# Attention by hash buckets and a gated spatial layer: new lengths and paces for the scheduler, and four heads by keys in place of two

## The chip, the core and the metric

The kernel runs on one core of one Trainium2 chip. Its engines are TensorE (PE, with its weight load PEld), VectorE (DVE), ScalarE (ACT), GpSimd (POOL) and SyncE (SP), which issues most of the DMAs. The metric is the device time of one execution in microseconds; lower is better. A profile is one execution taken by the hardware profiler; its span runs from the first to the last instruction of the program.

## The reference

Four batches, eight heads, 768 positions, 64 numbers per head. Each query and key gets a bucket from the signs of six projections, attention is allowed within a bucket, and the result goes through a feed-forward layer in which one half gates the other after a product over the positions.

```python
q_bits = (np.einsum('bhsd,dk->bhsk', q, proj) > 0)          # k likewise
mask = q_bucket[:, :, :, None] == k_bucket[:, :, None, :]
scores = scale * np.matmul(q, k.transpose(0, 1, 3, 2))
scores = np.where(mask, scores, -1000000000.0)
attn = softmax(scores)                                      # over the keys
x = (attn @ v).transpose(0, 2, 1, 3).reshape(B, S, H * D)   # B 4, S 768, H * D 512
h = np.maximum(x @ w_in, 0.0)                               # d_ff 1024
u, v = h[..., :512], h[..., 512:]
v_n = (v - mean(v)) / np.sqrt(var(v) + 1e-06)
v_s = np.einsum('ts,bsd->btd', w_spatial, v_n) + b_spatial[None, :, None]
return (u * v_s) @ w_out
```

## The kernel before

**Tiles and steps.** 32 heads make 16 pairs `p`, head `n = 2p + e`. A pair has six tiles of 128 positions, and a pair and a tile make one step `g`, 96 in all. `scores` issues the step's 16 matmuls (`sp`, L480): products of float16 halves and, last, the hash bits, which push scores outside the bucket down.

**A head by queries** (`by_queries`) has queries on the partitions. DVE copies the scores out with their row maximum (`low`, L509), ACT or POOL makes the bias (`bias`, `nb`), ACT takes the exponential (`exp`, L519) and rounds it to float16 (`half`, L523), DVE or POOL makes the rest in float16 (`rest`, L527), and a transpose by DMA on SP's queue turns the tile (`turn`, L531, `pt<-pp`) before `weighted` multiplies it with the values (`pv`, L637, 18 matmuls a tile).

**A head by keys** (`by_keys`, the heads in `WIDE`) has keys on the partitions: ACT takes the exponential from the scores in one go (L552), in float32, and `weighted` uses it as it stands (6 float32 products a tile, which the trace counts as 12 matmuls). There is no `low`, `half`, `rest` or transpose. But the maximum of each query has to be in the mask beforehand: `row_max` computes scores of the hashed float16 part once more on PE (`mx`, 24 matmuls a head), DVE reduces them (L584, 12 a head), `max_row` turns them on PE and moves them with a DMA of SP (L611, `hk<-mt`) into one row of the mask operand. The last four score matmuls of a pair's first step (`sp<-hk`) wait for that row.

**After a batch.** `normalize` scales a pair's result; a DMA transpose (L683, `xt<-xs`) turns it. When a batch's four pairs are done, `mlp_units` gives the feed-forward layer as groups of three matmuls each on PE: `vps` (v = x w_in), `ups` (u), `sps` (the product over positions), `ops` (the output). For the last batch `partial_units` (`vpp`, `upp`) does three of its pairs ahead of the fourth; `xp` is the PE transpose of the last pair. `weights()` loads and splits the layer's weights in 36 jobs, DMAs on SP's queue among them.

**What sets the order.** Every piece of work is an `Op` with an engine, a length `d`, a rank and what it waits for. `timetable` plays the whole program with these lengths: an engine that falls free takes the ready operation (ready within `LOOK`) of lowest rank. A tuple rank (step, x) goes before plain ranks; a plain rank below 8.9 counts from the current step, the feed-forward groups (9) come four steps behind. Scores of a step may not start before `begin`, which grows by `T_FIRST`, `T_KEYS`, `T_QUERIES` or `T_LAST` per step. Where PE would be idle for over 0.5 us, `fill` puts dummy matmuls (`warm`, L208) of 0.08 us each. `X` is added from one engine to the next, `LATE` and `LATE_D` before PE. Nothing of this runs on the chip: the outcome is one fixed sequence of instructions on each engine, and every engine takes its own in order.

```python
t = op("P", 1.5, go, *at["hl", p], *at["hk", p], on=[sc, held["hl", p], held["hk", p]], rank=(g, 0))
t.ready = begin
```

Of the kernel before, what the change touches and what calls it, by code (L numbers as in the profile page):

```python
# [14 lines left out]
ALU = mybir.AluOpType  # L15
# [3 lines left out]
P = 128  # L19
# [16 lines left out]
def lsh_attention_spatial_gating(  # L36
# [23 lines left out]
    WIDE = {4, 6}  # L60
# [14 lines left out]
    X = 0.15  # L75
    TURN = 1.92
    ops = []
# [27 lines left out]
    def op(e, d, fn, *after, on=(), rank=4, land=0.0, dma=0.0, need=None, gives=None, alone=False):  # L105
        o = Op(e, d, fn, rank, land, dma)
        o.need, o.gives, o.alone = need, gives, alone or "G" in e and fn.__name__ not in ("move", "bias")
        wait = [a for a in after if a is not None]
        for h in on:
            assert not h.closed  # L110
            if not h.users:
                wait += h.before
            h.users.append(o)
        for a in {id(a): a for a in wait}.values():
            a.then.append(o)
            o.left += 1
        return o
# [139 lines left out]
    def weights():  # L257
# [15 lines left out]
        for i, (src, dst, m, f, key) in enumerate(jobs):  # L273
            c = {}

            def fetch(src=src, m=m, i=i, c=c):
                if RB[i] < 2:
                    t = wk.tile([P, NF, HS], F16, tag=f"g{RB[i]}", name=f"raw{i}").rearrange("p a q -> p (a q)")
                else:
                    if i == 2:  # L280
                        st["raws"] = wk.tile([P, 2, S], F32, tag="u", bufs=UB, name="raws")
                    t = st["raws"][:, RB[i] - 2].bitcast(F16)
                c["raw"] = t[:, :m * (4 if src.dtype != F32 else 2)].bitcast(src.dtype)
                nc.sync.dma_start(out=c["raw"], in_=src)

            z = m / 256
            raw = buf(f"raw{RB[i]}", 1).new()
            hold_ = [raw] if RB[i] < 2 else [raw, raws]
            t = op("S", 0.6, fetch, on=hold_, dma=0.95 if src.dtype != F32 else 0.75, rank=R_W)
            t.ready = W_FROM - 6 + W_EVERY * i  # L290
            hold = hold_
            if src.dtype == F32:
                c["w"] = None
            else:
                def first(m=m, i=i, c=c):
                    raw = c["raw"]
# [52 lines left out]
    def urgent(p):  # L349

        return NT * p - (8 if keys(p) else 3)

    def hash_rows(p, *after):
# [22 lines left out]
        t = op("V", 0.62, bits, t, on=[g0], rank=(urgent(p), 2), gives="m")  # L376
        t = op("V", 0.3, scale, t, on=[g0, g1], rank=(urgent(p), 2), alone=True)
# [11 lines left out]
    def split_qk(p, *after):  # L389
# [3 lines left out]
        def high():  # L393
# [13 lines left out]
    def split_v(p, *after):  # L407
# [17 lines left out]
        at["vp", p] = op("V", 0.1 + 0.8 * z, low, t, on=[held["v", p], h], rank=(NT * p - 1, 4), alone=True)  # L425
# [57 lines left out]
    def scores(p, i, g, begin):  # L483
# [6 lines left out]
        t = op("P", 1.5, go, *at["hl", p], *at["hk", p], on=[sc, held["hl", p], held["hk", p]], rank=(g, 0))  # L490
# [5 lines left out]
    def by_queries(p, i, e, g, t, sc):  # L496
# [36 lines left out]
        t = op("V", 0.95, low, t, on=[sc, hx, held["nb", n], held["mr", n]], rank=(g, 0.1 + 0.1 * e))  # L533
        at["nb", n] = t = t1 = op("AG", BIAS, bias, t, on=[held["nb", n], held["mr", n]], rank=(g, 0.1 + 0.1 * e))
        t = op("A", 0.83, exp, t, on=[hx, held["nb", n]], rank=(g, 0.1 + 0.1 * e))
        t = op("A", 0.77, half, t, on=[hx, hp], rank=(g, 1 + e))
# [3 lines left out]
    def by_keys(p, i, e, g, t, sc):  # L540
# [21 lines left out]
        t = op("A", 0.75, exp, t, on=[sc, ht if wide_ else hx], rank=(g, 0.1 + 0.1 * e))  # L562
        if not wide_:
            t = op("A", 0.75, half, t, on=[hx, ht], rank=(g, 1 + e))
            t = t3 = op("VG", REST, rest, t, on=[hx, ht], rank=(g, 1 + e))
        at["pt", n, i] = t

    def row_max(p, i, c, *after):
# [8 lines left out]
        for e in ks:  # L577
# [8 lines left out]
            at["mx", 2 * p + e] = op("V", 0.55, high, t, on=[held["mx", 2 * p + e]], rank=R_MAX, gives="m")  # L586
# [55 lines left out]
    def normalize(n, g):  # L642
# [77 lines left out]
    POST = ("VG", (0.56, 1.0))  # L720
# [26 lines left out]
    def partial_units():  # L747
# [12 lines left out]
        for i in range(NT):  # L760
# [7 lines left out]
            def then(t, c, pool, i=i, copy=copy):  # L768
                at["vpart", i] = op("A", 0.5, lambda: copy(c), t, on=[hv_[i // 3]], rank=1, gives=pool)
# [11 lines left out]
    def mlp_units(b):  # L781
# [14 lines left out]
        def v_unit(i):  # L796
# [12 lines left out]
            def then(t, c, pool):  # L809
# [16 lines left out]
                if last:  # L826
                    t = op("V", 0.69, plus, t, at["vpart", i], on=[h, held["vpart"][i // 3]], rank=1, gives=pool)
                    t = op("A", 0.5, relu, t, on=[h], rank=1)
                else:
                    t = op("A", 0.5, relu, t, on=[h], rank=1, gives=pool)  # L830
                t = op("V", 0.9, stats, t, on=[h, hmv[i // 3]], rank=3)
# [7 lines left out]
        def norm(g, t):  # L839
# [22 lines left out]
            t = op("V", 0.6, newton, t, on=[hve, hr, hmv[g]], rank=3, alone=True)  # L862
            for j in range(3):
# [14 lines left out]
                z = op("A", 0.52, scale, t, on=[hv32[i], hve, hr], rank=3)  # L878
                z = op("A", 0.52, high, z, done.get("first"), on=[hv32[i], hvn[0]], rank=3)
                done.setdefault("first", z)  # L880
                done["vn", i] = op(*(("VG", (0.68, 1.17)) if last else ("G", 1.17)), low, z, on=[hv32[i], hvn[0]], rank=3)
# [3 lines left out]
        def u_unit(d, h):  # L885
# [9 lines left out]
            def then(t, c, pool):  # L895
# [9 lines left out]
                if part:  # L905
                    t = op("V", 0.54, plus, t, at["upart", d], on=[hu[h], held["upart"][d // 2]], rank=1, gives=pool)
                done["u", d, h] = op("A", 0.4, relu, t, done.get(("u", 0, h)), on=[hu[h]], rank=1, gives=None if part else pool)
# [3 lines left out]
        def s_unit(d, h):  # L911
# [7 lines left out]
            def then(t, c, pool):  # L919
# [14 lines left out]
                t = op("V", 0.55, first, t, at["bt"], on=[hy], rank=1, gives=pool)  # L934
# [9 lines left out]
        def o_unit(i):  # L944
# [5 lines left out]
            def then(t, c, pool):  # L950
# [6 lines left out]
                t = op("A", 0.5, copy, t, on=[ho], rank=1, gives=pool)  # L957
# [26 lines left out]
    W_FROM, W_EVERY = 20.0, 2.6  # L984
# [17 lines left out]
    for g in range(STEPS + LAG):  # L1002
# [101 lines left out]
```

## Time and profile before

| | us |
|---|---|
| median of 3 runs | 706.8 (703.88 to 711.1) |
| the profiled execution | 703.99 |
| its span | 702.2 |
| PE busy | 634.7 (90%), of it 56.0 in 825 `warm` matmuls |
| DVE busy | 519.7 (74%) |
| ACT busy | 502.4 (72%) |
| POOL busy | 271.5 (39%) |
| DMA queue of SP and ACT, 16 engines | 84.0% of the span |
| mean granted clock of PE | 0.983 |

Busy time counts from the first to the last moment of an instruction, without waiting; two instructions that overlap on an engine count once. [...] In a row of a group, behind the bar, stand the busy time in us, the mean length of one in ns, and the engine's idle time just before them with what ended it.

### The profile page before, as it was taken

The numbers are of one execution on the slowest core, as the hardware profiler recorded it, in microseconds if no ns is written. First come the engines' busy times: TensorE is split into PE (matmuls) and PEld (weight loads), VectorE is DVE, ScalarE is ACT, GpSimd is POOL, SyncE is SP. The second block draws the span as 40 slices with busy tenths as digits, with TensorE's granted clock in tenths as the row PEclk, the third lists the DMA queues.
The fourth block names the chain that finished last, engine by engine and source line by source line (L and its number), as shares of the span: only waits on it lengthen the run. The fifth ranks groups of instructions, "written<-read, shape, count | busy, mean of one in ns | idle before, by whom it ended". The sixth has DMA issues, their size and how long they took to land.

```text
span 702.2 us, 18439 instructions
## 1 busy us (share of the span) xinstructions
PE 634.7 (90%) x7475; PEld 394.9 (56%) x7475; DVE 519.7 (74%) x997; ACT 502.4 (72%) x822; POOL 271.5 (39%) x368
## 2 busy tenths in 40 slices
PE   5888699978879779899989899899999999999997
PEld 3565467765445565565555456564655565556553
DVE  5788697899687998887759787888897774255150
ACT  2879488888897889777757798878777994453212
POOL 4457645527742535581534262534152220010000
PEclk9989999999999899999999999999999999999999
DMA  6999996999999999999998999899989876000102
GB/s 194 190 194 189 212 180 149 200 187 217 204 213 215 188 215 155 187 193 180 190 192 143 198 195 203 154 220 161 232 167 177 146 123 107 0 31 16 46 1 90
DMA packets 326252, 113.29 MB, mean 161 GB/s; under 512 B 312984, under 2 KB 316056, under 8 KB 326168
## 3 DMA queue, kind: packets, MB, share of 16 engines
q1 hardware_dynamic: 322232, 110.98, 84.0%
q0 software_dynamic: 3840, 1.12, 0.9%
q8 instruction: 58, 0.95, 0.6%
q14 instruction: 26, 0.21, 0.1%
q10 hardware_dynamic: 96, 0.04, 0.0%
HBM read 27.94 MB, written 6.29 MB: 49 GB/s over the span
## 4 chain that ended last, share of the span: by engine, by line
PE 43%; ACT 19%; DMA 16%; DVE 9%; issue 8%; POOL 2%; SPq 2%; DVEq 0%; ACTq 0%; POOLq 0%
DMA pt<-pp 12%; PE sps L734 11%; ACT ex L519 7%; PE sp L480 7%; PE pv L637 7%; PE ops L734 7%; ACT pp L523 6%; DVE ex L509 5%; PE vps L734 4%; PE ups L734 3%; DVE pp L527 2%; PE vpp L734 2%; SPq L531 1%; POOL pp L527 1%; DMA raws<-w_sp 1%
## 5 line engine op out<-in xcount | busy, mean ns | idle before, releaser
L527 DVE TENSOR_TENSOR pp<-ex,pp 128x768 f16<-128x768 f32 x133 | 139.1, 1064 | 61.2 <-ACT pp L523 60.5
L519 ACT ACTIVATE ex<-ex,nb 128x768 f32<-128x768 f32 x180 | 167.5, 934 | 22.4 <-POOL nb L514 18.2
L509 DVE TENSOR_SCALAR_CACHE_REDUCE ex<-sp 128x768 f32<-128x768 f32 x180 | 165.3, 952 | 18.9 <-PE sp L480 14.0
L523 ACT CAST pp<-ex 128x768 f16<-128x768 f32 x180 | 144.6, 826 | 8.4 <-DMA pt<-pp 6.4
L637 PE MATMUL pv<-vp,pt 128*128 128x65 f16 x3240 | 126.3, 194 | 26.3 <-DMA pt<-pp 24.2
L637 PEld LDWEIGHTS <-pt 128*128 128x128 f16 x3240 | 112.8, 98 | 65.3 <-DMA pt<-pp 35.4
L480 PE MATMUL sp<-hl 64*128 64x384 f16 x1080 | 109.6, 328 | 13.8 <-DVE ex L509 13.0
L734 PE MATMUL sps<-ws,vn 128*128 128x384 f16 x576 | 102.4, 329 | 0.4 <-DVE sg L369 0.4
L527 POOL TENSOR_TENSOR pp<-ex,pp 128x768 f16<-128x768 f32 x47 | 77.5, 1655 | 39.6 <-ACT pp L523 32.8
L480 PEld LDWEIGHTS <-hl 64*128 64x128 f16 x1104 | 51.3, 95 | 62.2 <-issue 34.5
L514 POOL TENSOR_SCALAR nb<-mr 128x1 f32<-128x1 f32 x81 | 24.4, 301 | 142.7 <-DVE ex L509 115.7
L734 PEld LDWEIGHTS <-vn 128*128 128x128 f16 x576 | 54.2, 98 | 37.3 <-issue 4.5
L734 PE MATMUL ups<-xt,wi 128*128 128x384 f16 x348 | 63.9, 332 | 5.0 <-ACT vr L817 3.0
L734 PE MATMUL ops<-wo,g 128*128 128x512 f16 x288 | 66.5, 379 | 0.1
L384 POOL DMA_DIRECT2D hk<-sg x112 | 58.5, 529 | 16.1 <-issue 5.8
L734 PE MATMUL vps<-wi,xt 128*128 128x512 f16 x234 | 55.4, 379 | 2.1 <-ACT vr L817 2.1
L208 PE MATMUL warm<-ident 128*128 128x128 f16 x825 | 56.0, 224 | 0.0
L208 PEld LDWEIGHTS <-ident 128*128 128x128 f16 x825 | 48.7, 100 | 9.8 <-issue 9.3
L516 ACT ACTIVATE nb<-mr 128x1 f32<-128x1 f32 x99 | 19.4, 196 | 48.2 <-DVE ex L509 48.1
L734 PEld LDWEIGHTS <-wi 128*128 128x128 f16 x384 | 36.2, 99 | 29.5 <-issue 8.4
L480 PE MATMUL sp<-hk 63*128 63x384 f16 (+1 forms) x360 | 48.0, 327 | 4.5 <-DMA hk<-sg 1.8
L932 ACT CAST g<-sy 128x384 f16<-128x384 f32 x32 | 16.2, 508 | 41.4 <-DVE sy L936 41.1
(114 smaller groups left out, 743.1 us busy)
## 6 DMA issues: line engine op xcount, KB each, us to landing
qk<-kq SPq DMA_DIRECT2D x16, 768.0 KB
out<-o SPq DMA_DIRECT2D x24, 256.0 KB
v<-v SPq DMA_DIRECT2D x14, 384.0 KB
pt<-pp SPq DMA_TRANSPOSE x180
raw<-w_in SPq DMA_DIRECT2D x8, 256.0 KB
raws<-w_in SPq DMA_DIRECT2D x8, 256.0 KB
hk<-sg POOLq DMA_DIRECT2D x112, 9.0 KB, 3.6
raw<-w_sp SPq DMA_DIRECT2D x6, 192.0 KB
```

The source lines that it names most:

```text
L208: nc.tensor.matmul(b[:, :P], lhsT=ident, rhs=ident, start=True, stop=True)
L384: eng.dma_start(out=hkt(p)[D * e:D * e + 2 * NB, 1 - j // 2, (j % 2) * HS:(j % 2 + 1) * HS], in_=sg[1][32 * j + 16 * e:32 * j + 16 * e + 2 ...
L480: nc.tensor.matmul(ps[e][:, c - halves[0]], lhsT=src[r, l, rows], rhs=src[r, m, cs], start=(a == 0), stop=(a == len(passes) - 1))
L509: nc.vector.tensor_scalar(ex, st["sc", p, i][e], -float(2 ** 28), None, op0=ALU.max, op1=ALU.max, accum_out=st["mx", n][:, i:i + 1])
L514: nc.gpsimd.tensor_scalar(nb, mx, -ISQ, None, op0=ALU.mult)
L516: nc.scalar.activation(nb, mx, AF.Copy, scale=-ISQ)
L519: nc.scalar.activation(st["e32", n, i], st["e32", n, i], AF.Exp, bias=st["nb", n][:, i:i + 1], scale=ISQ)
L523: nc.scalar.copy(st["pp", n, i][:, 0], st["e32", n, i])
L527: eng.tensor_tensor(out=st["pp", n, i][:, 1], in0=st.pop(("e32", n, i)), in1=st["pp", n, i][:, 0], op=ALU.subtract)
L637: nc.tensor.matmul(o, lhsT=l, rhs=m, start=(i == 0 and k == 0), stop=(i == NT - 1 and k == len(todo_) - 1))
L734: nc.tensor.matmul(c[0], lhsT=l(), rhs=r(), start=(j == 0), stop=(j == len(products) - 1))
L932: nc.scalar.copy(gt[h][0][:, d], y[0])
```

## The change

- `WIDE` grows from heads 4 and 6 to heads 2, 4, 6 and 8: one head each of pairs 1 to 4, all in the first 30 steps.
- The lengths of nearly all operations are replaced. They were about the time an operation is busy; they are now the time until the engine's next operation (`low` 0.95 to 0.88, `half` 0.77 to 0.73, scores 1.5 to 1.42, weight products 0.55 to 0.47 and so on).
- The pace: `T_KEYS` 4.8 to 5.0, `T_QUERIES` 6.0 to 5.4, a new `T_THIRD` 6.1 for pairs 8 to 11, `T_LAST` 6.0 to 6.25, `START` 9.0 to 8.5.
- Weights: rank `R_W` 0.9 to 0.6 (a lower rank goes first), a job every 2.2 in place of 2.6. `R_QK`, `X`, `LATE`, `LATE_D` and `LOOK` change too.
- `LATER` shifts the rank of four kinds of operation by name: `relu`, `first`, `bias` and `turn`.
- `stats` now makes its tile when it is first needed, whichever of three tiles comes first.

```diff
-    WIDE = {4, 6}
+    WIDE = {2, 4, 6, 8}
...
-    X = 0.15
+    X = 0.14
     TURN = 1.92
+    LATER = {'relu': 0.1, 'first': -0.9, 'bias': -0.3, 'turn': 0.3}
...
     def op(e, d, fn, *after, on=(), rank=4, land=0.0, dma=0.0, need=None, gives=None, alone=False):
+        later = LATER.get(fn.__name__.strip("<>"), 0.0)
+        if not isinstance(rank, tuple):
+            rank = rank + later
+        elif rank[1]:
+            rank = (rank[0] + later, rank[1])
...
-        t = op("V", 0.95, low, t, on=[sc, hx, held["nb", n], held["mr", n]], rank=(g, 0.1 + 0.1 * e))
+        t = op("V", 0.88, low, t, on=[sc, hx, held["nb", n], held["mr", n]], rank=(g, 0.1 + 0.1 * e))
...
-                    if i % 3 == 0:
+                    if i // 3 not in mv:
...
-    T_FIRST, T_KEYS, T_QUERIES, T_LAST = 5.0, 4.8, 6.0, 6.0
-    START = 9.0
-    LOOK = 0.2
+    T_FIRST, T_KEYS, T_QUERIES, T_THIRD, T_LAST = 5.0, 5.0, 5.4, 6.1, 6.25
+    START = 8.5
+    LOOK = 0
     R_MAX = 0.3
-    R_QK = 0.95
-    REST, BIAS = (0.96, 1.68), (0.25, 0.25)
+    R_QK = 1.25
+    REST, BIAS = (0.88, 1.6), (0.22, 0.25)
     CROSS = {NP - 1}
-    R_W = 0.9
-    LATE, LATE_D = 0.5, 2.5
+    R_W = 0.6
+    LATE, LATE_D = 0.2, 2.0
...
-    W_FROM, W_EVERY = 20.0, 2.6
+    W_FROM, W_EVERY = 22.0, 2.2
...
-            begin += T_FIRST if p == 0 else T_KEYS if keys(p) else T_LAST if p >= NP - NPAIR else T_QUERIES
+            begin += T_FIRST if p == 0 else T_KEYS if keys(p) else T_LAST if p >= NP - NPAIR else T_THIRD if p >= NP - 2 * NPAIR else T_QUERIES
```

In the rows of the built order below, names carry their numbers: `pt1_4` is tile 4 of head 1, `sp8_0_0` the scores of pair 8, tile 0, first head, `sps0_0_0` a group of batch 0; the last number of a name only counts tiles.

SP's queue around the transposes of step 4 (`pt0_4`, `pt1_4`), before:

```order
L531 DMA_TRANSPOSE pt1_3_646<-pp1_3_557 128x12x128
L284 DMA raw4_690<-w_in 128x256
L332 DMA qk3_711<-kq 128x1536
L531 DMA_TRANSPOSE pt0_4_727<-pp0_4_649 128x12x128
L531 DMA_TRANSPOSE pt1_4_835<-pp1_4_685 128x12x128
L531 DMA_TRANSPOSE pt0_5_847<-pp0_5_749 128x12x128
L531 DMA_TRANSPOSE pt1_5_880<-pp1_5_772 128x12x128
L531 DMA_TRANSPOSE pt2_0_912<-pp2_0_870 128x12x128
```

And now:

```order
L537 DMA_TRANSPOSE pt1_3_604<-pp1_3_538 128x12x128
L537 DMA_TRANSPOSE pt0_4_638<-pp0_4_588 128x12x128
L537 DMA_TRANSPOSE pt1_4_697<-pp1_4_597 128x12x128
L338 DMA qk3_743<-kq 128x1536
L617 DMA ws1_80<-mt2_768 1x6x128
L537 DMA_TRANSPOSE pt0_5_794<-pp0_5_659 128x12x128
L537 DMA_TRANSPOSE pt1_5_854<-pp1_5_676 128x12x128
L290 DMA raw4_876<-w_in 128x256
```

The move of head 2's maxima (`ws1<-mt2`) is new and stands behind the transposes of step 4 and the load of pair 3 (`qk3`); a weight load and `qk3` no longer stand ahead of them, and pair 1 has one transpose a step (`pt3_0` without `pt2_0`).

SP's queue where the last weights (`w_sp`, `w_out`) are loaded, before, around steps 32 and 33 (heads 10 and 11):

```order
L284 DMA raw29_3419<-w_out 128x256
L284 DMA raws_311<-w_sp 128x384
L284 DMA raw32_3428<-w_out 128x256
L531 DMA_TRANSPOSE pt10_2_3439<-pp10_2_3417 128x12x128
L531 DMA_TRANSPOSE pt11_2_3466<-pp11_2_3425 128x12x128
L284 DMA raws_311<-w_out 128x256
L284 DMA raws_311<-w_sp 128x384
L683 DMA_TRANSPOSE xt4_3595<-xs4_3503 128x12x128
L531 DMA_TRANSPOSE pt10_3_3618<-pp10_3_3528 128x12x128
L531 DMA_TRANSPOSE pt11_3_3662<-pp11_3_3552 128x12x128
```

And now, around steps 26 to 28 (head 9 alone):

```order
L290 DMA raws_338<-w_sp 128x384
L290 DMA raw29_2573<-w_out 128x256
L290 DMA raw32_2598<-w_out 128x256
L689 DMA_TRANSPOSE xt3_2618<-xs3_2569 128x12x128
L537 DMA_TRANSPOSE pt9_2_2656<-pp9_2_2575 128x12x128
L290 DMA raws_338<-w_out 128x256 x2
L537 DMA_TRANSPOSE pt9_3_2715<-pp9_3_2680 128x12x128
L290 DMA raw33_2750<-w_out 128x256
L338 DMA qk6_2754<-kq 128x1536
L351 DMA v32_6_2781<-v 128x768
```

The last weight loads moved from among the transposes of two heads by queries to among those of one.

PE where the first group of the product over positions (`sps0_0_0`) begins, before: its first six matmuls stand ahead of step 48 (`sp8_0_0`); the last of them are

```order
L734 LDWEIGHTS vn0_0_4846
L734 MATMUL sps0_0_0_5095<-ws1_80,vn0_0_4846 128x384
L734 LDWEIGHTS vn0_1_4847
L734 MATMUL sps0_0_0_5095<-ws0_79,vn0_1_4847 128x384
L480 LDWEIGHTS hl8_4434
L480 MATMUL sp8_0_0_5106<-hl8_4434 128x384
```

And now, ahead of step 43 (`sp7_1_0`):

```order
L740 LDWEIGHTS vn0_0_3626
L740 MATMUL sps0_0_0_4114<-ws1_80,vn0_0_3626 128x384
L740 LDWEIGHTS vn0_1_3627
L740 MATMUL sps0_0_0_4114<-ws0_79,vn0_1_3627 128x384
L486 LDWEIGHTS hl7_3446
L486 MATMUL sp7_1_0_4119<-hl7_3446 128x384
```

The group starts five steps earlier. Over the whole order PE has these matmuls, counted in the same three parts (before, and after the change):

| | up to step 47 | steps 48 to 95 | behind the last scores |
|---|---|---|---|
| `warm` | 636, 178 (and 64, 66 ahead of step 0) | 69, 37 | 56, 18 |
| `mx` | 48, 96 | 0, 0 | 0, 0 |
| `pv` in float16 | 1422, 1206 | 1710, 1728 | 108, 90 |
| key tiles (`pv` in float32) | 12, 24 | 0, 0 | 0, 0 |
| `vps` and `vpp` | 72, 72 | 144, 162 | 72, 54 |
| `ups` and `upp` | 96, 96 | 162, 192 | 126, 96 |
| `sps` | 6, 72 | 282, 306 | 288, 198 |
| `ops` | 0, 0 | 144, 180 | 144, 108 |

More of the change, by code (lines that the diff above doesn't have):

```diff
@@ L375, in hash_rows @@
         t = op("P", 0.8, go, at["qk", p], *after, on=[qk], rank=(urgent(p), 3), need=("m", 1))
-        t = op("V", 0.62, bits, t, on=[g0], rank=(urgent(p), 2), gives="m")
-        t = op("V", 0.3, scale, t, on=[g0, g1], rank=(urgent(p), 2), alone=True)
+        t = op("V", 0.54, bits, t, on=[g0], rank=(urgent(p), 2), gives="m")
+        t = op("V", 0.24, scale, t, on=[g0, g1], rank=(urgent(p), 2), alone=True)
         at["hk", p] = []
@@ L424, in split_v @@
         t = op("A", 0.15 + 0.6 * z, high, at["v", p], *after, on=[held["v", p], h], rank=(NT * p - 1, 4))
-        at["vp", p] = op("V", 0.1 + 0.8 * z, low, t, on=[held["v", p], h], rank=(NT * p - 1, 4), alone=True)
+        at["vp", p] = op("V", 0.07 + 0.8 * z, low, t, on=[held["v", p], h], rank=(NT * p - 1, 4), alone=True)
     def mean_v(p, *after):
@@ L768, in then @@
             def then(t, c, pool, i=i, copy=copy):
-                at["vpart", i] = op("A", 0.5, lambda: copy(c), t, on=[hv_[i // 3]], rank=1, gives=pool)
+                at["vpart", i] = op("A", 0.49, lambda: copy(c), t, on=[hv_[i // 3]], rank=1, gives=pool)
             group(f"vpp{i}", F2, v_products(b, i, pairs), then, on, after, bank_m, rank=8.9)
@@ L861, in norm @@
             t = op("A", 0.45, root, t, on=[hve, hr], rank=3)
[L862 removed]
+            t = op("V", 0.67, newton, t, on=[hve, hr, hmv[g]], rank=3, alone=True)
             for j in range(3):
@@ L876, in low @@
                     eng.tensor_tensor(out=vn[1][:, i], in0=v32[i], in1=vn[0][:, i], op=ALU.subtract)
-                z = op("A", 0.52, scale, t, on=[hv32[i], hve, hr], rank=3)
+                z = op("A", 0.7, scale, t, on=[hv32[i], hve, hr], rank=3)
                 z = op("A", 0.52, high, z, done.get("first"), on=[hv32[i], hvn[0]], rank=3)
                 done.setdefault("first", z)
-                done["vn", i] = op(*(("VG", (0.68, 1.17)) if last else ("G", 1.17)), low, z, on=[hv32[i], hvn[0]], rank=3)
+                done["vn", i] = op(*(("VG", (0.6, 1.12)) if last else ("G", 1.12)), low, z, on=[hv32[i], hvn[0]], rank=3)
         hu, hg, gs = {}, {}, {}
@@ L905, in then @@
                 if part:
-                    t = op("V", 0.54, plus, t, at["upart", d], on=[hu[h], held["upart"][d // 2]], rank=1, gives=pool)
-                done["u", d, h] = op("A", 0.4, relu, t, done.get(("u", 0, h)), on=[hu[h]], rank=1, gives=None if part else pool)
+                    t = op("V", 0.48, plus, t, at["upart", d], on=[hu[h], held["upart"][d // 2]], rank=1, gives=pool)
+                done["u", d, h] = op("A", 0.38, relu, t, done.get(("u", 0, h)), on=[hu[h]], rank=1, gives=None if part else pool)
             group(f"ups{b}_{d}_{h}", HS, u_products(b, d, h, LASTP if part else ALLP), then, xts, ready + at["wu"], bank(), [hu[h]], 8.9 if last else 9)
@@ L932, in high @@
                     nc.scalar.copy(gt[h][0][:, d], y[0])
-                t = op("V", 0.55, first, t, at["bt"], on=[hy], rank=1, gives=pool)
+                t = op("V", 0.5, first, t, at["bt"], on=[hy], rank=1, gives=pool)
                 either = lambda o: nc.gpsimd if o.e == "G" else nc.vector
@@ L955, in copy @@
                     nc.scalar.activation(o[0], c[0], AF.Copy, scale=1.0 / (SX * SX))
-                t = op("A", 0.5, copy, t, on=[ho], rank=1, gives=pool)
+                t = op("A", 0.49, copy, t, on=[ho], rank=1, gives=pool)
                 op("S", 0.4, lambda: nc.sync.dma_start(out=out[b, i * P:(i + 1) * P, :], in_=o[0]), t, on=[ho], rank=2, dma=0.95)
```

48 lines of the change are left out of this document (24 added, 24 removed).

## The prediction

> **What bounds the kernel now.** The page of the profile comes first: how long the span is, and which engines the chain that ended last runs through.
>
> ```profile
> span 702.2 us, 18439 instructions
> PE 43%; ACT 19%; DMA 16%; DVE 9%; issue 8%; POOL 2%; SPq 2%; DVEq 0%; ACTq 0%; POOLq 0%
> ```
>
> No engine carries even half of the chain, so one bound for the whole span would be wrong. I therefore cut the span where the limits change. A step is one query tile of one pair of heads: 16 score matmuls, 96 steps. Counting those matmuls in the timeline of PE gives the first matmul of steps 0, 6 and 48 and the first and last rows of step 95:
>
> ```profile
> 12.76 1.15 PE L480 MATMUL sp<-hl 64*128 64x384 f16 x12
> 43.53 0.66 PE L480 MATMUL sp<-ws 64*128 64x384 f16 x6
> 289.61 0.32 PE L480 MATMUL sp<-hl 64*128 64x384 f16 x1 [1.44 <-DVE ex L509]
> 574.62 1.15 PE L480 MATMUL sp<-hl 64*128 64x384 f16 x12
> 575.61 0.49 PE L480 MATMUL sp<-hk 63*128 63x384 f16 x4
> ```
>
> Third, the view of windows, cut at those places (columns: stretch, length, busy time of PE, PEld, DVE, ACT, POOL, granted clock, DMA share, GB/s):
>
> ```profile
> 12.76:289.61 276.85, 231.87 (x3257) 160.79 (x3255) 231.84 (x456) 225.45 (x386) 147.84 (x187) 0.96 1.03 193
> 289.61:576.03 286.42, 274.21 (x3335) 160.66 (x3335) 230.22 (x431) 228.11 (x350) 114.83 (x162) 0.99 1.00 181
> 576.03:702.20 126.17, 121.64 (x808) 68.59 (x806) 48.95 (x99) 45.33 (x85) 5.04 (x5) 1.00 0.17 41
> ...
> 84.32:137.10 52.78, 49.41 (x625) 37.00 (x624) 42.91 (x92) 40.70 (x73) 27.71 (x33) 1.00 0.89 184
> 137.10:174.06 36.96, 31.72 (x460) 22.04 (x459) 35.87 (x66) 32.88 (x61) 16.75 (x22) 1.00 1.06 202
> 174.06:289.61 115.55, 94.35 (x1330) 62.03 (x1329) 96.97 (x188) 97.97 (x168) 57.89 (x77) 0.96 1.07 197
> ```
>
> Before step 48 DMA is the fullest resource (share 1.03), DVE is at 84% and ACT at 81%, and much of PE's 232 us is warm-up filler. From step 48 to the last scores PE is busy 274.2 of 286.4 us. After them PE is busy 121.6 of 126.2 us and DMA lies idle: 121.6 us of PE work stand in a tail that overlaps nothing else. In the last three rows the two pairs that have a key head today (steps 12 to 23) take 52.8/12 = 4.4 us a step at DMA share 0.89. The four pairs behind them take 6.2 and 6.4 us a step at 1.06 and 1.07.
>
> **Prices.** PE's prices come from the chain of waits, where a merged row gives the time per instruction:
>
> ```profile
> 73.15 0.78 PE hp L362 x8
> 98.06 1.48 PE pv L637 x12
> 103.75 0.65 PE mx L480 x4
> 481.89 1.20 PE pv L637 x36
> 619.23 1.79 PE warm L208 x32
> 643.77 7.80 PE ups L734 x48
> 651.58 7.77 PE ops L734 x36
> 659.34 17.55 PE sps L734 x108
> ```
>
> So: `mx`, `ups` and `sps` 0.163 us each, `ops` (and `vps`, `vpp`, equally wide) 0.216, `pv` 0.033, warm 0.056, and 1.48 us for the weighted sum of one key tile. The other engines' prices come from the groups, DMA's from the issues of the transposes (minimum, median, maximum ns):
>
> ```profile
> L519 ACT ACTIVATE ex<-ex,nb 128x768 f32<-128x768 f32 x180 | 167.5, 934 | 22.4 <-POOL nb L514 18.2
> L509 DVE TENSOR_SCALAR_CACHE_REDUCE ex<-sp 128x768 f32<-128x768 f32 x180 | 165.3, 952 | 18.9 <-PE sp L480 14.0 <-PE mx L480 3.7 <-POOL pp L527 0.8
> L523 ACT CAST pp<-ex 128x768 f16<-128x768 f32 x180 | 144.6, 826 | 8.4 <-DMA pt<-pp 6.4
> L527 DVE TENSOR_TENSOR pp<-ex,pp 128x768 f16<-128x768 f32 x133 | 139.1, 1064 | 61.2 <-ACT pp L523 60.5
> L584 DVE TENSOR_REDUCE mx<-mx 128x1 f32<-128x384 f32 x24 | 12.3, 548 | 0.6 <-PE mx L480 0.4
> L552 ACT ACTIVATE ex<-sp 128x768 f32<-128x768 f32 x12 | 9.7, 804 | 8.5 <-PE sp L480 8.5
> L531 SPq DMA_TRANSPOSE pt<-pp x180: 1317/1738/4457, 23.4 to 584.9; - x180
> ```
>
> **Part one, up to step 48.** Heads 2 and 8 go over to keys, so 12 tiles lose their `low`, `half`, `rest` and transpose. DVE saves 12 × 0.918 (165.3/180) and 8 × 1.06 us, and gains 24 maxima of 0.51: 7.2 us less. ACT loses 12 × (0.93 + 0.80), gains 12 × 0.81 and drops small biases: about 13 us less. DMA loses 12 transposes of 1.74 us: 20.9 us less. On PE the built order has, up to step 48: 48 more `mx` (+7.8), 12 key tiles more (+17.8) against 216 fewer `pv` (-7.2), 66 more `sps` (+10.7), 458 fewer warm matmuls (-25.6): +3.5 us in all, so real work takes the filler's place. Weight loads leave the queue by step 29 instead of step 38, so the stretch from 174 us on, the one with share 1.07, keeps only transposes and head loads.
>
> How much comes through? If DMA is the bound, all 20.9 us. If DVE is, then 7.2 less what comes early behind the 66 `sps` (3.7 evictions and their products, about 1.3 us each): 2.4 us. DMA's share of 1.03 against DVE's 0.84 is the stronger row, so I take 18 us for steps 6 to 47. The Trainium skill, page "DMA: Bandwidth & Descriptors", section "Latency and other measured facts", gives 261 GB/s for a DMA transpose: an estimate of 1.5 us for the 393 KB of one tile, and 18 us for twelve where the row's median makes 20.9. No run here shows a transpose alone, and the median of the row stands in the sum.
>
> Against that, step 6 gets a wait that only steps 12 and 18 have today: its mask needs the key head's maxima, moved through SP's queue. Today's wait at step 12 shows its size:
>
> ```profile
> 43.70 8.92 DMA pt<-pp
> ...
> 78.76 3.32 SPq L531
> 82.84 4.23 DMA hk<-mt
> ...
> 87.11 0.50 PE L480 MATMUL sp<-hk 64*128 64x384 f16 x4 [1.64 <-DMA hk<-mt]
> ```
>
> In the new order the scores of step 6 stand behind the weighted sums of step 4, whose transpose was issued at 43.70 and took 8.9 us, and the mask's move stands behind that transpose and a 768 KB load. Queued behind the waiting matmul are all scores of pair 1, hence ACT's and DVE's next work. With two loads fewer ahead of it I put step 6 at 50 us instead of 43.5: 6.5 us lost; 0 if the transposes land in 2 us, 9 with all of that landing. Step 48: 289.6 - 18 + 6.5 = 278.1, between 268.7 (289.6 - 20.9) and 296 (289.6 + 6.5).
>
> **Part two, steps 48 to 95.** The order has 36 more `ops` (+7.8), 24 more `sps` (+3.9), 30 more `ups` (+4.9), 18 `vpp` (+3.9), 18 `pv` (+0.6) and 32 fewer warm (-1.8): +19.3. PE's 274.2 becomes 293.5. Idle was 12.2 us; denser PE work covers more waits, so I take 9, bounds 4 and 12: 302.5 us, 297.5 to 305.7.
>
> **Part three, the tail.** What went forward is gone here: 90 `sps` (-14.6), 36 `ops` (-7.8), 30 `ups` (-4.9), 18 `vpp` (-3.9), 18 `pv` (-0.6), 38 warm (-2.1), so 121.6 becomes 87.7; 4.5 us of idle stay. But there is less to cover the last softmax:
>
> ```profile
> 576.97 3.35 SPq L531 DMA_TRANSPOSE pt<-pp  x2
> 583.39 3.28 SPq L531 DMA_TRANSPOSE pt<-pp  x2
> 591.51 0.71 PE L637 MATMUL pv<-vp,pt 128*128 128x65 f16 x18
> 594.33 0.50 PE L704 MATMUL xp<-ident,xs 128*128 128x128 f16 x6
> ```
>
> From the last scores (576.0) to `xp` (594.3) are 18.3 us; the new order has 90 `pv`, 36 `vpp` and 24 `upp` between them, 3.0 + 7.8 + 3.9 = 14.7 us. I add 3 us of new wait: 95.3 us, 92 to 99.
>
> **The small edits** (`LATER`, `LOOK`, `X`, new lengths) only choose among instructions that are ready; they remove none. I cost them at nothing, because in parts two and three PE's other matmuls hide the choice; where that cover is thin, up to step 48, their worth is inside the 2.4 to 20.9 us above, and below nothing it is the first rival.
>
> **Sum.** 278.1 + 302.5 + 95.3 = 675.9 us of span. The profiled execution took 703.99 us, 1.8 over its span: 677.7. The median shown, 706.8, is 1.004 times that execution: 680.
>
> **Rivals**, all on the median's scale.
>
> *DVE and ACT hold the first part.* Step 48 stays at 289.6: 12 us more, 692. For it: both are above 80% busy, in-order, and both already wait for one another; against it: the share of DMA, and 4.4 us a step where a key head runs. Chance 0.17.
>
> *All of DMA's relief comes through and step 6 loses nothing*: 268.7 + 299 + 93 + 1.8 = 662.5, times 1.004: 665. For it: the quick steps 12 to 23; against it: the landing of 8.9 us ahead of step 6. Chance 0.10.
>
> *PE's clock.* 458 of 636 filler matmuls go from part one, and where fill was thin the clock dipped:
>
> ```profile
> 30.00:40.00 10.00, 7.39 (x87) 5.44 (x89) 7.53 (x17) 9.02 (x13) 4.28 (x8) 0.66 1.09 202
> 230.00:240.00 10.00, 7.04 (x103) 5.11 (x104) 8.67 (x21) 8.79 (x17) 4.59 (x5) 0.66 0.80 176
> ```
>
> A dip costs 10 × 0.34 = 3.4 us of PE time. Seven more of them where PE is the bound give 680 + 24 = 704, no change. Against it: `sps` and key tiles now stand where the filler stood, and both dips lie where PE is not the bound. Chance 0.09. The Trainium skill, page "TensorE: Matmul & The Clock Gate", section "Part 1: The HAM clock gate", states that a window of about 3.4 us without enough matmul work puts the clock to half; the two rows agree (0.66 over 10 us is 6.8 us at half), and by that rule filler removed without replacement speaks against this change.
>
> *Slower: the key heads' starts.* Four pairs now begin with a mask that comes through maxima, a transpose on PE, a copy and SP's queue. If each start holds PE's in-order queue for 10 us (3.3 + 4.2 us above plus the copy), with nothing to make up for it, the four cost 40 us in place of the 6.5 I counted and part one gains nothing from its lighter load: 278 becomes about 316 and the time 718. It decides from some 27 us above my step 48, a time over 707. Against it: today step 12 waits 1.64 us at the mask itself and steps 12 to 23 then run at 4.4 us each. Chance 0.09.
>
> **Chances.** The forecast 0.55, the rivals 0.17, 0.10, 0.09, 0.09. About 1% (7 us) is what a measurement can tell from no change, so under 699.7 is faster. Faster: 0.55 + 0.17 + 0.10 = 0.82, of which I move 0.02 to same, for a first rival that comes with long waits in part two. Same: 0.11. Slower: 0.09. The range goes from just below the second rival, 663, to the upper bounds of parts one and two (296 + 305.7 + 99 + 1.8, times 1.004: 705); it leaves out the slow case and what lies at its ends.
>
> **What would show it.** Step 48's first scores near 278 us, step 6's near 50; DMA share under 1 up to about 170 us; PE busy over 96% from step 48 on; about 95 us after the last scores, with one wait of 2 to 4 us ahead of `xp`. A first matmul of step 48 after 300 us, or a tail above 105 us, would show me wrong.

## The result, and the profile after

The changed kernel takes 671.5 us (median; 669.12 to 673.13), the kernel before on the same chip 708.0 (703.88 to 711.1). The ratio is 0.9485, 95% interval 0.9426 to 0.9544: faster by 5.1%, where 680 us, a ratio of 0.962 (680/706.8), were forecast. The profiled execution took 673.13 us with a span of 671.4.

The page's span and chain, as they stand now:

```profile
span 671.4 us, 17301 instructions
PE 47%; DVE 16%; ACT 14%; DMA 13%; issue 6%; POOL 3%; SPq 1%; DVEq 0%; ACTq 0%; POOLq 0%
```

The first score matmul of steps 0, 6 and 48, and the last scores, in the timeline of PE:

```profile
14.12 1.15 PE L486 MATMUL sp<-hl 64*128 64x384 f16 x12
49.46 0.82 PE L486 MATMUL sp<-ws 64*128 64x384 f16 x8
283.56 1.15 PE L486 MATMUL sp<-hl 64*128 64x384 f16 x12
577.39 1.15 PE L486 MATMUL sp<-hl 64*128 64x384 f16 x12
578.38 0.49 PE L486 MATMUL sp<-hk 63*128 63x384 f16 x4
```

And the windows cut there, with the columns of the prediction's windows (stretch, length, busy PE, PEld, DVE, ACT, POOL, granted clock, DMA share, GB/s); the last four rows cut the first one up again, behind step 6, at steps 12, 24 and 30. The granted clock is the mean share of its full clock that PE was given; the share of DMA adds up the times of all packets, so it can pass 1:

```profile
14.12:283.56 269.44, 240.26 (x2846) 157.01 (x2846) 224.53 (x467) 216.26 (x375) 154.73 (x193) 0.94 0.93 180
283.56:578.80 295.24, 289.91 (x3431) 168.89 (x3430) 229.40 (x436) 232.81 (x355) 111.31 (x165) 1.00 1.00 181
578.80:671.40 92.60, 87.81 (x578) 48.93 (x576) 40.10 (x85) 36.54 (x68) 3.10 (x4) 0.99 0.17 42
...
49.46:80.08 30.62, 27.47 (x302) 18.50 (x301) 25.60 (x62) 20.98 (x38) 15.00 (x15) 0.89 0.82 169
80.08:149.72 69.64, 63.97 (x663) 44.78 (x662) 55.21 (x128) 49.91 (x93) 38.31 (x53) 0.88 0.84 167
149.72:180.76 31.04, 27.01 (x334) 19.52 (x333) 23.46 (x43) 28.42 (x53) 21.16 (x27) 1.00 0.87 202
180.76:283.56 102.80, 93.70 (x1164) 55.39 (x1163) 90.88 (x180) 90.03 (x150) 53.75 (x69) 0.98 1.04 185
```

Step 48 comes 6.0 us earlier (283.6 against 289.6), the stretch from there to the last scores is 8.8 us longer (295.2 against 286.4), and the tail is 33.6 us shorter (92.6 against 126.2): 30.8 us in all. PE's idle time in the middle stretch fell from 12.2 to 5.3 us. So the gain lies in the tail: PE does, while attention runs, much of what it used to do alone at the end. Attention itself ends 2.8 us later than before.

### The profile page after: what moved, and what is told of

Its sections match the earlier page's. It is cut to its first block, busy times and chain, and to the rows that moved or that the text cites. A ratio compares the mean times of both kernels' runs of the same rounds, so it can differ in the third digit from the quotient of the medians.

```text
span 671.4 us, 17301 instructions
## 1 busy us (share of the span) xinstructions
PE 626.3 (93%) x6931; PEld 381.0 (57%) x6931; DVE 502.7 (75%) x1000; ACT 489.1 (73%) x800; POOL 272.9 (41%) x375
## 4 chain that ended last, share of the span: by engine, by line
PE 47%; DVE 16%; ACT 14%; DMA 13%; issue 6%; POOL 3%; SPq 1%; DVEq 0%; ACTq 0%; POOLq 0%
PE sp L486 10%; PE pv L643 8%; PE sps L740 8%; PE ops L740 7%; DMA pt<-pp 7%; PE vps L740 5%; DVE ex L515 5%; ACT ex L525 4%; ACT pp L529 4%; DVE pp L533 3%; PE ups L740 3%; PE vpp L740 2%; DMA raw<-w_sp 2%; DVE hl L408 2%; PE mx L486 1%
## 5 line engine op out<-in xcount | busy, mean ns | idle before, releaser
L533 DVE TENSOR_TENSOR pp<-ex,pp 128x768 f16<-128x768 f32 x125 | 125.5, 1012 | 63.5 <-ACT pp L529 62.8
L515 DVE TENSOR_SCALAR_CACHE_REDUCE ex<-sp 128x768 f32<-128x768 f32 x168 | 154.7, 952 | 22.9 <-PE sp L486 22.8
L525 ACT ACTIVATE ex<-ex,nb 128x768 f32<-128x768 f32 x168 | 155.9, 933 | 12.5 <-POOL nb L520 9.6
L529 ACT CAST pp<-ex 128x768 f16<-128x768 f32 x168 | 137.4, 827 | 7.8 <-DMA pt<-pp 5.2
L643 PEld LDWEIGHTS <-pt 128*128 128x128 f16 x3024 | 107.7, 98 | 46.2 <-issue 21.5
L643 PE MATMUL pv<-vp,pt 128*128 128x65 f16 x3024 | 120.4, 194 | 7.1 <-DMA pt<-pp 7.1
L533 POOL TENSOR_TENSOR pp<-ex,pp 128x768 f16<-128x768 f32 x43 | 71.2, 1660 | 59.3 <-ACT pp L529 40.3
L486 PEld LDWEIGHTS <-hl 64*128 64x128 f16 x1116 | 53.3, 96 | 59.6 <-issue 32.3
L740 PEld LDWEIGHTS <-g 128*128 128x128 f16 x288 | 26.7, 98 | 31.0 <-issue 1.9
L740 PEld LDWEIGHTS <-xt 128*128 128x128 f16 x288 | 25.9, 98 | 30.3 <-issue 2.5
L643 PE MATMUL pv<-vf,ex 128*128 128x65 f32 x288 | 37.9, 283 | 3.3 <-ACT ex L558 3.2
```

Source lines behind the costliest of these rows:

```text
L486: nc.tensor.matmul(ps[e][:, c - halves[0]], lhsT=src[r, l, rows], rhs=src[r, m, cs], start=(a == 0), stop=(a == len(passes) - 1))
L515: nc.vector.tensor_scalar(ex, st["sc", p, i][e], -float(2 ** 28), None, op0=ALU.max, op1=ALU.max, accum_out=st["mx", n][:, i:i + 1])
L525: nc.scalar.activation(st["e32", n, i], st["e32", n, i], AF.Exp, bias=st["nb", n][:, i:i + 1], scale=ISQ)
L529: nc.scalar.copy(st["pp", n, i][:, 0], st["e32", n, i])
L533: eng.tensor_tensor(out=st["pp", n, i][:, 1], in0=st.pop(("e32", n, i)), in1=st["pp", n, i][:, 0], op=ALU.subtract)
L643: nc.tensor.matmul(o, lhsT=l, rhs=m, start=(i == 0 and k == 0), stop=(i == NT - 1 and k == len(todo_) - 1))
```

## What the runs were to tell apart

Theory 1 is the prediction's: the time is the start of step 48, plus PE's work from there on, plus what the order leaves behind the last scores. The rivals put the gain elsewhere: in the load that the two key heads take off DMA, DVE and ACT; in the paces; in nothing that the small edits do. A second question is the part of the sum that was uncertain from the start, what bounds steps 6 to 47.

The experiments with their median time, and the same terms read from each profile, in us. The last column is worked out from the built order alone: the matmuls behind the last scores at the prediction's prices, filler included, with 4.5 us of idle added. The medians come from three chips, on which the kernel before took 708.0, 707.3 and 706.0; ratios, below, are each to the runs of before on the same chip.

| | median | step 6 | step 48 | 48 to last scores | tail | tail from the order |
|---|---|---|---|---|---|---|
| before | 706.0 to 708.0 | 43.5 | 289.6 | 286.5 | 126.1 | 126 |
| changed | 671.5 | 49.5 | 283.6 | 295.3 | 92.5 | 92 |
| heads alone | 722.6 | 55.8 | 275.2 | 289.8 | 155.4 | 153 |
| two heads | 704.1 | 42.8 | 283.3 | 298.1 | 117.4 | 116 |
| without `LATER` | 677.7 | 57.7 | 280.1 | 296.8 | 103.2 | 103 |
| old paces | 675.1 | 53.3 | 285.8 | 287.8 | 102.1 | 101 |
| old margins | 696.7 | 52.2 | 273.4 | 297.7 | 123.0 | 120 |
| no filler | 674.9 | 48.4 | 284.7 | 295.5 | 92.4 | 91 |
| three heads | 685.8 | 42.7 | 282.9 | 296.0 | 103.8 | 103 |
| slower paces | 683.7 | 49.7 | 286.4 | 304.6 | 89.6 | 88 |

## Heads alone, and two heads with everything else

Heads alone: the kernel before with one line changed.

```diff
-    WIDE = {4, 6}
+    WIDE = {2, 4, 6, 8}
```

> The kernel before with heads 2, 4, 6 and 8 by keys and nothing else changed. Theory 1 (the gain is PE work that leaves the tail for the attention part): the old lengths and paces leave even more behind the last scores, 148 us of matmuls instead of 121; with part two near 278 us (its 265 us of PE work and 12 of idle) and step 48 near 283, the span is about 713 us, no faster than before. Rival (the gain is the load that the two heads take off DMA, DVE and ACT): the span falls to about 680 us.

Measured: 722.57 us, ratio 1.0215 (1.0186 to 1.0243), slower than before. Its windows from step 48 to the last scores, and behind them:

```profile
275.17:564.98 289.81, 272.56 (x3504) 169.29 (x3502) 238.17 (x430) 222.34 (x350) 108.71 (x150) 0.99 1.00 181
564.98:720.36 155.38, 149.07 (x958) 82.69 (x957) 54.66 (x120) 59.04 (x111) 11.44 (x10) 1.00 0.15 39
```

Attention ends 11.1 us earlier than before (565.0), so the heads do take load off. But with the old lengths and paces PE still has 17 us of idle between step 48 and the last scores, and 149 us of matmuls stand behind them. The load that was saved went into an earlier end of attention and a longer tail. The rival, which took the saved load to be the gain, forecast 680. Theory 1's own 713 was 7 us short of the span, 720.4: step 48 came 7.8 us earlier than put, the stretch behind it was 11.8 us longer and the tail 3.4.

Two heads: the changed kernel with the opposite edit.

```diff
-    WIDE = {2, 4, 6, 8}
+    WIDE = {4, 6}
```

> The changed kernel with heads 4 and 6 alone by keys; lengths, paces and ranks as in the change. Theory 1: 111 us of matmuls stand behind the last scores, tail 116 us, part two 286 + 5 us, step 48 at 283 to 290: 690 to 697 us, so the lengths and paces alone are worth 5 to 12 us and the rest needs both. Rival (the heads are the gain): about 700 us or more, no different from before.

Measured: 704.05 us, ratio 0.997 (0.9931 to 1.0009): no difference from before that can be told. That is what the rival said of the time; theory 1's 690 to 697 us were too low, and so was its claim that lengths and paces alone bring 5 to 12 us. The terms show where it fell short: the tail is 117.4 us where 116 were put, and step 48 comes at 283.3, as with four heads (283.6), but the stretch between them is 298.1 us where 291 were put.

So neither half of the change gains anything alone, and both together gain 5.1%. The reading that fits is that the two heads free time on DVE, ACT and DMA in the first 30 steps, and that the new lengths, paces, ranks and margins together let the plan fill such time with groups of the feed-forward layer. The counts bear it out: behind the last scores stand 198 `sps` matmuls in the changed kernel, 276 with two heads and 297 with the heads alone. Ranks, paces and margins are put back one at a time below; no run puts the old lengths back by themselves, so their own share is not shown.

## The small edits: ranks, paces, margins

Without the shifted ranks:

```diff
-    LATER = {'relu': 0.1, 'first': -0.9, 'bias': -0.3, 'turn': 0.3}
+    LATER = {}
```

> The changed kernel without the four shifted ranks. Theory 1: 98 us of matmuls behind the last scores instead of 87.5, part two 288 + 5 us, step 48 unchanged near 283: about 679 us, 8 us over the changed kernel. Rival (the small edits cost and bring nothing): within 2 us of it, 671.

Measured: 677.74 us, ratio 0.9568 (0.9535 to 0.9602) against 0.9485 (0.9426 to 0.9544). The intervals touch, so that the ranks are worth 6 us is likely rather than shown. The tail is shown: 103.2 us, 103 worked out, 10.7 more than in the changed kernel, while step 48 comes 3.5 us earlier.

The old paces:

```diff
-    T_FIRST, T_KEYS, T_QUERIES, T_THIRD, T_LAST = 5.0, 5.0, 5.4, 6.1, 6.25
-    START = 8.5
+    T_FIRST, T_KEYS, T_QUERIES, T_THIRD, T_LAST = 5.0, 4.8, 6.0, 6.0, 6.0
+    START = 9.0
```

> The changed kernel with the old paces and start (4.8, 6.0, 6.0 and 9.0), new lengths kept. Theory 1: 97 us of matmuls behind the last scores, tail 101 us, part two 279 us of PE work and 8 of idle, step 48 at 283 to 290: 671 to 678 us, near the changed kernel, since the lengths rather than the pace move the work. Rival (the pace is the gain): 690 us or more.

Measured: 675.08 us, ratio 0.9523 (0.9459 to 0.9587), in the range of theory 1 and not to be told from the changed kernel. 9.6 us more tail stand against 7.5 us less between step 48 and the last scores. The rival, that the pace is the gain, falls.

The old margins that the scheduler adds between engines, and the old `LOOK`:

```diff
-    X = 0.14
-    LOOK = 0
-    LATE, LATE_D = 0.2, 2.0
+    X = 0.15
+    LOOK = 0.2
+    LATE, LATE_D = 0.5, 2.5
```

> The changed kernel with the old X (0.15), LOOK (0.2), LATE and LATE_D (0.5, 2.5). Theory 1 (the tail is what the order leaves behind the last scores): 116 us of matmuls there, tail 120 us, part two 277 us of PE work and 5 of idle, step 48 near 283: 685 us of span, 14 over the changed kernel, so these margins are worth nearly half of the gain. Rival (the small edits are worth nothing): within 3 us of the changed kernel.

Measured: 696.73 us, ratio 0.9882 (0.9824 to 0.994), 25 us over the changed kernel. The tail is 123.0 us, and PE stays idle for 14.6 us where the changed kernel has 5.3:

```profile
273.38:571.13 297.75, 283.20 (x3411) 166.14 (x3409) 227.03 (x424) 230.18 (x361) 124.49 (x166) 0.99 0.97 177
571.13:694.09 122.96, 116.34 (x754) 64.87 (x753) 48.30 (x98) 42.44 (x78) 2.94 (x4) 1.00 0.15 41
```

Against the expectation the tail is 3 us longer, and the stretch ahead of it has 10 us more idle time and 6 us more PE work; step 48 in turn comes 10 us earlier than put, and also 10 us earlier than in the changed kernel. The 72 `sps` that the changed kernel does ahead of step 48 all stand behind it here. Of the edits that leave the heads alone these four constants, put back together, weigh most; none of them is an instruction. That wide margins make the plan take PE's matmuls of the layer to be ready later than they are is how the scheduler's code reads; which of the four does it was not tried.

## Step 6 and three heads

```diff
-    WIDE = {2, 4, 6, 8}
+    WIDE = {4, 6, 8}
```

> The changed kernel with heads 4, 6 and 8 by keys: pair 1 goes back to two heads by queries, so step 6 has no mask to wait for. Theory (step 6's wait costs 6.5 us and the order decides the rest): step 6 near 43.5, but 99 us of matmuls behind the last scores, tail 103 us, part two 286 + 5 us, step 48 near 283: 677 us of span. Rival (the wait at step 6 is carried through to the end): step 48 near 277 and 671 us or less.

Measured: 685.82 us, ratio 0.9709 (0.9676 to 0.9743). Step 6, without a mask to wait for, starts here:

```profile
42.71 1.58 PE L486 MATMUL sp<-ws 64*128 64x384 f16 x13
```

That is 6.8 us earlier than in the changed kernel (49.46), where the prediction priced the wait at 6.5. In the changed kernel the last four score matmuls of step 6 then wait for the mask once more, which the prediction did not count:

```profile
53.49 0.82 PE L486 MATMUL sp<-ws 64*128 64x384 f16 x4 [2.89 <-DMA ws<-mt]
```

Yet step 48 comes at 282.9, 0.7 us earlier than with the wait, because steps 6 to 47 take 240.2 us here and 234.1 with head 2 by keys: what that head relieves about pays for its wait. The tail is 11.3 us longer, since with one head less by keys the order puts less of the layer ahead of the last scores. The rival (step 48 near 277, 671 us or less) falls. The forecast of 677 us was 5.7 short of the span, 682.7; 5 of it lie between step 48 and the last scores (296.0 instead of 291).

## The filler and the clock

All warm-up matmuls left out:

```diff
-                fill.append((free[e], int((gap - 0.1) / 0.08)))
+                pass
```

> The changed kernel with no warm-up matmuls at all (365 fewer). Theory (filler is free time on PE where it stands, and the clock matters little): within 3 us of the changed kernel. Rival (the filler keeps PE's clock up): more stretches at half clock up to step 48, granted clock under 0.96, step 48 later by 8 us or more, 680 us or more.

Measured: 674.88 us, ratio 0.9548 (0.9514 to 0.9582), not to be told from the changed kernel, though the medians differ by 3.4 us where the theory said 3 at most. No `warm` matmul is left in its trace; the changed kernel has 299 (178, 66, 37 and 18 by the table ahead of the prediction), not the expectation's 365. The clock falls as the rival said, the time much less. The window from step 0 to step 48:

```profile
9.78:284.71 274.93, 237.49 (x2670) 150.84 (x2667) 223.52 (x470) 216.29 (x375) 153.42 (x194) 0.91 0.91 179
```

A clock of 0.91 over 274.9 us is 24.7 us of clock pulses that PE was not given, against 16.2 (0.94 of 269.4) in the changed kernel and 11.1 (0.96 of 276.9) before. Without filler ahead of it step 0 starts 4.3 us earlier, the stretch up to step 48 is 5.5 us longer, and step 48 comes 1.1 us later. The rival's 8 us and 680 us are not reached. But the early start hides most of what the stretch lost: 8.5 us more of missing pulses go with 5.5 us more of time, so this run does not show that the clock is free up to step 48.

## What bounds steps 30 to 47

The changed kernel needs 102.8 us for these 18 steps. Four kernels add one engine's work there, unknown to the scheduler, and leave what is computed as it is. The edits:

```diff
-            nc.scalar.copy(st["pp", n, i][:, 0], st["e32", n, i])
+            for _ in range(2 if 5 <= p <= 7 and e == 0 else 1):
+                nc.scalar.copy(st["pp", n, i][:, 0], st["e32", n, i])
```

> The changed kernel, with the rounding to float16 done twice for the first head of pairs 5 to 7: 18 more ACT instructions of 0.83 us, 15 us, unknown to the scheduler. From step 30 to step 48 the changed kernel takes 102.8 us (ACT busy 90.0, DVE 90.9, PE 93.7, DMA share 1.04). Theory (DMA bounds this stretch, as the forecast took it): under 5 us longer. Rival (the in-order engines, ACT and DVE, bound it together): 8 to 15 us longer.

```diff
-            nc.vector.tensor_scalar(ex, st["sc", p, i][e], ...
+            for _ in range(2 if 5 <= p <= 7 and e == 0 else 1):
+              nc.vector.tensor_scalar(ex, st["sc", p, i][e], ...
```

> The changed kernel, with the copy of the scores done twice for the first head of pairs 5 to 7: 18 more DVE instructions of 0.92 us, 16.6 us. Steps 30 to 47 took 102.8 us. Theory (DMA bounds): under 5 us longer. Rival (ACT and DVE bound it): 8 to 17 us longer.

```diff
         def turn():
+            if 5 <= p <= 7 and e == 0:
+                nc.sync.dma_start(out=out[B - 1, i * P:(i + 1) * P, :], in_=bt[:, :DM])
```

> The changed kernel, with one more store of 256 KB ahead of each transpose of the first head of pairs 5 to 7 (18 stores into rows of the output that the last batch writes later). At the 185 GB/s of this stretch 18 stores are 25 us of DMA; 17 us at the scheduler's price. Theory (DMA bounds steps 30 to 47): 17 to 25 us longer than 102.8. Rival (ACT and DVE bound it and DMA has room): under 8 us.

```diff
+            for _ in range(3 if 5 <= p <= 7 else 0):
+                sums(ps, p, slice(i * P, (i + 1) * P), ALL[:1], False)
             sums(ps, p, slice(i * P, (i + 1) * P), ALL, False)
```

> The changed kernel, with the first pass of the scores issued three times more in pairs 5 to 7: 12 more matmuls a step, two at a time, 1.0 us, 17.6 us in 18 steps. PE is busy 93.7 of 102.8 us there. Theory (DMA bounds): PE's 9 us of room take half of it, 8 to 10 us longer. Rival (PE waits on ACT and DVE, and its room lies in pieces that cannot be used): 14 to 18 us longer.

Steps 30 to 47 in the four, in the order ACT, DVE, DMA, PE:

```profile
179.64:290.99 111.35, 97.61 (x1164) 56.58 (x1162) 88.40 (x179) 102.85 (x166) 52.77 (x69) 0.95 0.95 172
```

```profile
182.97:299.10 116.13, 101.36 (x1165) 58.67 (x1163) 103.08 (x211) 89.37 (x149) 53.34 (x69) 0.93 0.89 165
```

```profile
179.27:291.07 111.80, 97.12 (x1165) 56.16 (x1163) 91.75 (x182) 92.55 (x153) 54.16 (x70) 0.96 1.09 212
```

```profile
182.98:293.45 110.47, 108.54 (x1380) 65.26 (x1378) 89.62 (x180) 91.03 (x151) 53.97 (x70) 1.00 0.95 175
```

ACT: 15 us added, 8.5 longer. DVE: 16.6 added, 13.3 longer. DMA: 18 stores of 256 KB (25 us at 185 GB/s), 9.0 longer. PE: 17.6 added by the expectation, 14.8 more busy, 7.7 longer. The whole kernels took 682.1, 688.0, 679.9 and 683.6 us. ACT and DVE lie in the rival's ranges and above the theory's 5 us. DMA passes on 9 of 17 to 25 us, less than the theory and a little more than the rival allowed, and all but 1.8 us of it in the last six steps (41.2 us in place of 34.0). So DMA did not bound this stretch as the forecast took it: it had room for about half of the stores or more. Its share of 1.04 is no sign of a full queue; with the stores it rose to 1.09, and the rate from 185 to 212 GB/s. PE's load came out just under the theory's 8 us, which tells nothing, since any bound outside PE leaves it that room.

No load comes out at nothing and none in full, so the chain goes from engine to engine. DVE passes on the most, but that it is the tightest is not shown: the granted clock was 0.93 in its run where the changed kernel has 0.98, 8.1 us of missing pulses in place of 2.1, while PE's run had 1.00. The four runs did not hold the clock fixed, and they rest on one profile each: steps 0 to 29, which no edit touched, end between 179.3 and 183.0 us.

## A slower pace

```diff
-    T_FIRST, T_KEYS, T_QUERIES, T_THIRD, T_LAST = 5.0, 5.0, 5.4, 6.1, 6.25
+    T_FIRST, T_KEYS, T_QUERIES, T_THIRD, T_LAST = 5.0, 5.0, 5.8, 6.3, 6.4
```

> The changed kernel with the paces 5.8, 6.3 and 6.4 in place of 5.4, 6.1 and 6.25, which puts still more of the layer ahead of the last scores: 83.5 us of matmuls behind them. Theory 1: tail 87 us, part two 291.5 + 5 us, step 48 at 286: 669.5 us, level with the changed kernel since PE is full from step 48 on. Rival (every matmul taken from the tail is a gain): 666 us or less.

Measured: 683.74 us, ratio 0.9682 (0.9643 to 0.9722), 12 us over the changed kernel. Both forecasts fail. The tail is the shortest of all, 89.6 us, 2.9 under the changed kernel, but the stretch ahead of it is 9.3 us longer:

```profile
286.43:591.06 304.63, 294.49 (x3527) 173.12 (x3527) 239.62 (x442) 231.55 (x357) 106.01 (x159) 1.00 0.98 174
```

PE is busy 4.6 us longer than in the changed kernel there and idle for 10.1 us in place of 5.3. What a matmul leaves in the tail it costs again ahead of it, once PE is full, and this slower pace added idle time on top. No kernel tried here beats the changed one.

## Why the prediction was right, and where it was off

**Direction and cause: right.** The forecast added a start of step 48, PE's work behind it and a tail; the measured span is 671.4 against 675.9, and the gain is the shorter tail (33.6 us, forecast 30.9), as forecast. That the sum came within 4.5 us is partly luck: part one was 5.5 us too low, parts two and three 7.3 and 2.7 too high. The median lies 8.5 us under the forecast of 680; the other 4 us are the factor of 1.004, since this time the profiled execution is above the median (673.13 against 671.5). The chance of 0.80 lay on faster.

**Part one: the sum right within 5.5 us, one term mis-sized.** Forecast 278.1, measured 283.6. Step 6 was put at 50 and came at 49.46, 6.8 us behind the kernel with three heads. The term that failed is "I take 18 us for steps 6 to 47": they take 234.1 us instead of 246.1, a gain of 12.0. Nor does the gain lie where the transposes went away. These are the windows of steps 6 to 29, which lost all twelve: before, changed, and with the heads alone (columns as above).

```profile
43.53:174.06 130.53, 112.35 (x1584) 81.01 (x1582) 112.38 (x227) 103.80 (x184) 71.58 (x87) 0.99 1.02 193
49.46:180.76 131.30, 118.45 (x1294) 82.80 (x1292) 104.27 (x232) 99.31 (x183) 74.47 (x93) 0.91 0.84 176
55.85:161.95 106.10, 100.27 (x1203) 72.92 (x1201) 90.43 (x200) 82.78 (x140) 58.90 (x77) 1.00 0.86 158
```

With the heads alone these steps are 24.4 us shorter, at a full clock, though they begin 12.3 us later and have 11 weight loads on SP's queue in place of 17. Step 48 of that kernel comes 14.4 us earlier than before (275.2), with 48 `ups` fewer ahead of it, where the prediction's 18 us of relief less 6.5 of wait make 11.5. So relief of about the forecast size is there when the two heads come by themselves. In these steps of the changed kernel none of it is left: 30 weight loads stand in these steps, and a clock of 0.91 means 11.8 us of missing pulses instead of 1.3, at a PE that is busy for 90% of the stretch. The gain is all in steps 30 to 47 (102.8 instead of 115.6), which lost no transpose and keep 2 weight loads of 14. So the step that failed took the relief whole and put the earlier weight loads and the lower clock of steps 6 to 29 at nothing in its sum. How the loss divides between these two, and whether they are all of it, no run shows. DMA as the one bound of the first part does not hold either (the added loads above); its rival, DVE and ACT hold the first part, put step 48 at 289.6, 6.0 us too late.

**The price of one transpose.** Its row reads almost as before, so the median of 1.7 us was a fair price of the issue. How much of it was time on the path no run shows by itself.

```profile
L537 SPq DMA_TRANSPOSE pt<-pp x168: 1273/1683/4147, 21.4 to 585.4; - x168
```

**Part two: idle mis-sized.** 302.5 forecast, 295.2 measured, 2.3 below the lower bound. PE's work was put at 293.5 and is 289.9; the idle time at 9 and is 5.3. Denser work covered more waits than allowed; the slower pace and the old margins, with 10.1 and 14.6 us of idle, show how much of that hangs on the order.

**The tail: right within 3 us.** 95.3 forecast, 92.6 measured. PE's 87.7 us are 87.8. The extra wait of 3 us ahead of `xp` did not come. The chain of waits after the last scores:

```profile
588.38 0.55 PE pv L643 x18
588.93 1.46 PE upp L740 x9
590.40 0.55 PE pv L643 x18
590.94 2.44 PE upp L740 x15
593.38 0.35 PE xp L710 x6
593.73 0.02 issue
593.75 0.81 ACT xt L715
594.56 0.04 issue
594.60 0.49 PE xp L710 x6
```

`xp` starts 14.5 us after the last scores, as long as the 14.7 us of work that the order puts between them. The last transpose is issued 6.5 us after the last scores (585.4 in the row above) where it took 8.8 before (584.9), which fits with the shorter cover being still long enough.

**The small edits: wrong as it stands.** "I cost them at nothing" is contradicted by the old margins, which cost 25 us when put back. The sum did not suffer, because the counts of matmuls were taken from the built order, and the edits' work was already in them. Their worth is in the order, and no trace of before can price them one by one.

**The clock.** The rival's mechanism is there: 16.2 us of missing pulses up to step 48 instead of 11.1, and 24.7 without filler. The prediction set it aside because the dips of before lie where PE is not the bound; that premise failed. Between 85.45 and 98.5 us of the changed kernel the chain that ended last runs through PE alone, from 86.8 us on at half its clock (five of these us stand in the last section), so some 5 us are lost on the path there, about as much as step 48 came late. That the one makes the other is not shown. The rival's 704 us are far off all the same. The rule of the Trainium skill that the prediction named (page "TensorE: Matmul & The Clock Gate", section "Part 1: The HAM clock gate") has the clock at half after a window without enough matmul work, and the granted clocks of 0.94 and, without any filler, 0.91 agree; that PE then stays at half for 10 busy us does not follow from it, and here the measurement decides. As an argument against this change the rule is not borne out.

**The slower rival, key heads' starts.** It did not come: step 48 is at 283.6, and the start at step 6 costs 6.8 us and 2.9 at the mask. Its sum was wrong as it stands: 40 us in place of 6.5 give a step 48 of 312, or of 330 without the 18 us of relief, not 316.

## What to carry to other kernels

Where a program ends in work of one engine alone, count that engine's instructions behind the last step of the other work in the built order: here that count gave the tail within 3 us in each of the nine kernels of the table that were built after it, while a DMA share over 1 misled on what bounds. Relief on busy engines can be worth nothing until the order is made again with it: the two heads alone made the kernel 2% slower, all the other edits without them changed nothing, both together gained 5%. And a scheduler's margins between engines can weigh as much as instructions: the old four constants, among them 0.3 and 0.5 us more ahead of PE, cost 25 us here.

## What was not expected of the hardware

PE's clock stayed at half for longer than the waits ahead of it lasted, while PE was busy all the time. The window of the changed kernel in which that shows:

```profile
90.00:100.00 10.00, 10.00 (x65) 5.92 (x66) 4.43 (x12) 5.50 (x11) 4.05 (x5) 0.50 0.92 163
```

Four `mx` take 1.4 us there and a key tile 2.75, in the chain of waits of the same place, against 0.65 and 1.48 in the prediction's rows:

```profile
88.00 1.39 PE mx L486 x4
89.39 2.75 PE pv L643 x12
92.14 1.37 PE mx L486 x4
```

The waits ahead of it were 0.45 and 1.64 us. What released the clock, or why ten busy microseconds did not, was not tried.
